# Batch 0's keys in three tiles of 128 and one shared by both heads, instead of four of 112

## The chip, the cores and the metric

The kernel runs on one core of a Trainium2 chip. The metric is the device time of one execution, in microseconds, lower being better. The core has five engines that run their own instructions in order and wait for each other by semaphores: TensorE (PE, matmuls into the PSUM banks; its weight loads are listed as PEld), VectorE (DVE), ScalarE (ACT), GpSimd (POOL) and SyncE (SP), whose queue starts nearly all DMAs.

## What is computed

An attention with soft-capped scores over 4 batches of 12 heads, 448 positions and 64 columns, and behind it two feed-forward layers over the 1792 tokens. All of it is in float32; the cap that comes with the inputs is 30.

```python
def _attn_ref(q, k, v, cap):
    scale = 1.0 / np.sqrt(q.shape[-1])
    scores = scale * np.matmul(q, k.transpose(0, 1, 3, 2))
    scores = cap * np.tanh(scores / cap)
    scores = scores - np.max(scores, axis=-1, keepdims=True)
    attn = np.exp(scores)
    attn = attn / (np.sum(attn, axis=-1, keepdims=True) + 1e-09)
    return np.matmul(attn, v)
...
x = attn_out.transpose(0, 2, 1, 3).reshape(B * S, H * D)
h = x @ moe_w_in                       # 768 to 2048
g = np.where(h >= 1, h, np.where(h <= -1, 0.0, (h + 1) ** 2 / 4))
x = g @ moe_w_out                      # 2048 to 768
h = np.maximum(np.maximum(x @ w1, x @ w2), x @ w3)
return h @ w_out                       # 768 to 768
```

## The kernel before

**Two arms.** Every engine loads the cap's bits into a register (`values_load`, L211) and compares them with a limit (L228). For a cap over 32 the arm with `keep_max=True` runs, which takes the row maxima off the scores; it stands directly behind the comparison. For smaller caps, as here, the arm with `keep_max=False` runs. It has no maxima, stands behind the whole first arm, and is reached by a taken branch of each engine. Each arm holds the full program, over 2,500 rows of it on PE.

**Order of the work.** Inside an arm everything is first noted as operations with a cost, a due time and the buffers they use; the class `Plan` then puts them in an order by these costs and due times, and `emit` writes the instructions in that order. An engine's queue is therefore fixed when the program is built. `slots` says how many buffers each pool has: "u" holds tiles of 896 columns (qk, tanh and exp tiles, sums), "h" those of 448, "v", "wf" (weights as float32) and "raw" (weights as they come) their own; in PSUM there are two score banks "s" (`ps_s`, two banks wide), one "a" and three "m".

**Attention of a pair of heads** (`attention(b, i, ...)`, L571 on, six pairs per batch). SP loads q and k of both heads (`load_heads`, two DMAs of 224 KB) and v (`load_v`, L580, one DMA of 224 KB, 1 KB in a row per key and head). The 448 keys are cut into four tiles of 112. For batch 0 a score tile is four plain float32 matmuls (`score`, L616, matmul in L624): 64 and 48 keys of each head, in four corners of the array at once. ACT turns both heads' scores into tanh (L631, 112x896) and later into exp (L678). DVE adds the four exp tiles into one, `se` (L718, by the helper in L313); PE multiplies that by ones into `ps_r` (`total4`, L707, four products of 224 columns; the last pair uses `total`, L693). PE weighs v with the exp tiles into `ps_a` (`weigh`, L834): four tiles of four products with 32 columns each. For batches 1 to 3 (`FULL`) q and k are divided into two parts each, and a score tile is six faster products (L613).

**Reciprocals.** The row sums leave `ps_r` on DVE or ACT (`rs`, L765 or L763). For all pairs but the last, POOL starts a DMA that gathers them into a small tile `rc` (L786), DVE takes 896 reciprocals there (L807), SP writes them to DRAM (L789) and reads them back, spread over the partitions, into `rs` (L794, two DMAs). Then DVE multiplies `ps_a` by `rs` into `xf` (L313), which frees the bank of `ps_a`, and divides `xf` into two parts `x`. The last pair takes its reciprocals on DVE in four pieces (L818).

**The bank of `ps_a`** is chosen by this line:

```python
pa = buf("m" if first and i % 2 else "a", "ps_a", [P, 512])
```

For batch 0 (`first`) pairs 0, 2 and 4 take the only "a" bank, pairs 1, 3 and 5 one of the three "m" banks, which `ps_r` uses too.

**Feed-forward.** The first layer of batch 0 multiplies `xf` with the first six weight tiles in plain float32 (`PLAIN`, L892), later ones in three products of divided parts (L897 to L899). The weights come as 64-bit words (`raw`, 768 KB a tile) and are turned into float32 by four operations on DVE or ACT (L410 to L437); SP stores them for later use (L443). Attention of batch 1 is mixed into the feed-forward of batch 0, and so on. The last two batches and layers run through L1115.

Of the kernel before, what the change touches and what calls it, by code (L numbers as in the profile page):

```python
# [18 lines left out]
LIMIT_BITS = 0x42000000  # L19

# [184 lines left out]
def kernel(  # L205
# [21 lines left out]
    consts = const, qk0, cap_sb, ones, qscale  # L227
    with tc.If((bits & 0x7FFFFFFF) > LIMIT_BITS) as test:  # L228
# [14 lines left out]
def softcap_attention_two_ffn(  # L243
# [19 lines left out]
    D = 64  # L263
# [7 lines left out]
    FULL = (1, 2, 3)  # L271
    RC = 16
# [11 lines left out]
    slots = {"u": 35, "h": 9, "v": 3, "w": 4, "wf": 5, "raw": 3, "rc": 2, "s": 2, "a": 1, "m": 3}  # L284
    const, qk0, cap_sb, ones, qscale = consts
    dram = pool("dram", 1, space=bass.MemoryType.DRAM)
    pools = {n: pool(n, slots[n]) for n in ("u", "h", "v", "w", "wf", "raw", "rc")}
# [9 lines left out]
    def half(name):  # L297
        return buf("h", name, [P, S])
# [214 lines left out]
    halves = {}  # L513
    def combine(layer, m, run, want):
# [50 lines left out]
    def attention(b, i, begin, last):  # L565
# [7 lines left out]
        vt = buf("v", "v", [C, 2, NCH, D])  # L573
        early = first and i == 0
        qkt = [plan.fixed(qk0) if early else unit("qk")]
        t = [unit("t", rows=C) for _ in range(NCH)]
        if keep_max:
            mx, mb = unit("mx", rows=C), unit("mb", rows=C)
# [27 lines left out]
        for c in range(NCH):  # L606
            ps = buf("s", "ps_s", [P, 2, 512])

            def score_full(e, c=c, ps=ps):
                for n, (k, q) in enumerate(parts3):  # L610
                    for j in range(2):
                        o = slice(j * D, (j + 1) * D)
                        nc.tensor.matmul(  # L613
                            ps.tile[:C, j, :S], k.tile[o, 1, c * C : (c + 1) * C],
                            q.tile[o, 0], start=n == 0, stop=n == 2,
                        )  # L616

            def score(e, c=c, ps=ps):

                for k in (0, D):  # L620
                    n = min(D, C - k)
                    for j in range(2):
                        o = slice(j * D, (j + 1) * D)
# [987 lines left out]
```

## Time and profile before

| | us |
|---|---|
| median of 3 runs | 963.65 |
| lowest and highest run | 961.59, 967.66 |
| the profiled execution | 961.39 |
| its span, first to last recorded instruction | 959.6 |
| PE busy in the span | 939.0 |
| DVE busy | 776.7 |
| ACT busy | 597.2 |

The profile is one execution. The busy time of an engine counts its instructions, not its branches or the starting of DMAs. A float32 matmul stands as two records, so a score tile of four matmuls is "x8". The granted clock (PEclk) is a share of PE's full 2.4 GHz. Idle time of an engine other than the one that sets the pace costs nothing by itself.

### The profile page before, as it was taken

Reading aid. Unit: us, or ns where it says so; the run is one execution under the profiler, and the core shown is the slowest. Engines: PE = TensorE matmul, PEld = TensorE weight load, DVE = VectorE, ACT = ScalarE, POOL = GpSimd, SP = SyncE. Lnnn points to the kernel's source line nnn. Section 1 sums busy time; section 2 is a strip of 40 time slices with the busy share of each in tenths; the row PEclk is TensorE's granted clock in tenths of the full one; section 3 lists DMA queues with packets and bytes.
Section 4 is the critical chain, followed back from the end, with each engine's and each line's share of the span. In section 5 each row is a group of like instructions: output and inputs, shape, how many; then the busy total and the mean of one; then the engine's idle time right before and its main releaser. Section 6 shows DMA issues by size and latency. Waiting matters only on the chain.

```text
span 959.6 us, 14758 instructions
## 1 busy us (share of the span) xinstructions
PE 939.0 (98%) x5323; PEld 755.9 (79%) x5323; DVE 776.7 (81%) x1285; ACT 597.2 (62%) x935; POOL 14.5 (2%) x27
## 2 busy tenths in 40 slices
PE   6889999999999999999999999999999999999998
PEld 1125777777776767677999999999999999899997
DVE  2789898888898898789989848787889869858782
ACT  6798898774989887875434315566874825332441
POOL 0000000000000000000000000000000000000000
PEclk9799999999999999999999999999999999999999
DMA  6667767989998998953777887432333336446344
GB/s 178 208 187 222 236 187 236 268 254 319 304 276 275 270 305 267 270 149 127 251 269 249 294 285 271 151 113 83 104 102 106 110 106 211 130 150 206 101 144 136
DMA packets 95340, 194.49 MB, mean 203 GB/s; under 512 B 12094, under 2 KB 56858, under 8 KB 95258
## 3 DMA queue, kind: packets, MB, share of 16 engines
q1 hardware_dynamic: 94378, 193.36, 64.3%
q8 instruction: 44, 0.72, 0.3%
q14 instruction: 38, 0.31, 0.1%
q0 software_dynamic: 736, 0.10, 0.1%
q10 hardware_dynamic: 144, 0.00, 0.0%
HBM read 142.51 MB, written 50.81 MB: 201 GB/s over the span
## 4 chain that ended last, share of the span: by engine, by line
PE 91%; issue 4%; DMA 2%; DVE 2%; ACT 1%; POOL 0%; POOLq 0%; DVEq 0%; ACTq 0%
PE ps_m L1115 32%; PE ps_s L1115 11%; PE ps_m L897 10%; PE ps_m L899 9%; PE ps_m L898 9%; PE ps_a L834 6%; PE ps_s L613 5%; PE ps_a L1115 5%; PE ps_m L892 3%; PE ps_r L707 1%; DMA rc<-rs 1%; DVE op L313 1%; PE ps_s L624 1%; DMA rc<-rc 0%; DMA qk<-in_qk 0%
## 5 line engine op out<-in xcount | busy, mean ns | idle before, releaser
L1115 PE MATMUL ps_m<-op,w 128*128 128x448 f32 x1575 | 324.1, 365 | 0.5 <-DVE M L313 0.5
L1115 PEld LDWEIGHTS ps_m<-op,w 128*128 128x128 f32 x1575 | 295.6, 188 | 24.5 <-DVE M L313 0.9
L313 DVE TENSOR_TENSOR w<-wf,w 128x512 fp32r<-128x512 f32 (+2 forms) x155 | 117.3, 760 | 13.7 <-ACT w L308 11.4
L308 ACT ACTIVATE w<-wf 128x512 fp32r<-128x512 f32 (+2 forms) x124 | 84.2, 682 | 63.8 <-PE ps_m L1115 30.7
L631 ACT ACTIVATE t<-ps_s,qscale 112x896 f32<-112x896 f32 x96 | 92.7, 1004 | 32.1 <-PE ps_s L613 22.5
L1115 PE MATMUL ps_s<-op,w 128*128 128x448 f32 x522 | 110.7, 366 | 0.4 <-DVE op L313 0.2
L1115 PEld LDWEIGHTS ps_s<-op,w 128*128 128x128 f32 x522 | 98.0, 188 | 8.7 <-ACT op L308 0.5
L678 ACT ACTIVATE t<-t,cap_sb 112x896 f32<-112x896 f32 x96 | 96.4, 1040 | 0.3
L308 ACT ACTIVATE w<-ss 128x384 fp32r<-128x384 f32 (+1 forms) x93 | 53.1, 583 | 64.9 <-PE ps_m L1115 37.4
L834 PE MATMUL ps_a<-t,v 112*32 112x448 f32 (+1 forms) x752 | 83.0, 569 | 1.1 <-DVE xf L313 0.6
L897 PE MATMUL ps_m<-g,w 128*128 128x448 f32 x192 | 72.8, 379 | 0.0
L313 DVE TENSOR_TENSOR w<-ss,w 128x384 fp32r<-128x384 f32 (+1 forms) x98 | 59.7, 626 | 14.4 <-ACT w L308 14.0
L899 PE MATMUL ps_m<-g,w 128*128 128x448 f32 x192 | 70.4, 367 | 0.0
L898 PE MATMUL ps_m<-g,w 128*128 128x448 f32 x192 | 70.3, 366 | 0.0
L834 PEld LDWEIGHTS ps_a<-t,v 112*32 112x32 f32 (+1 forms) x752 | 23.3, 113 | 48.5 <-issue 37.6
L437 DVE SCALAR_TENSOR_TENSOR wf<-raw 128x768 int32<-128x768 int32 (+1 forms) x64 | 55.0, 860 | 5.7 <-ACT raw L429 4.6
L421 DVE SCALAR_TENSOR_TENSOR raw<-raw 128x768 int32<-128x768 int32 (+1 forms) x64 | 55.2, 863 | 4.8 <-ACT raw L410 4.1
L897 PE MATMUL ps_m<-x,w 128*128 128x448 f32 x156 | 58.7, 376 | 0.0
L899 PE MATMUL ps_m<-x,w 128*128 128x448 f32 x156 | 57.0, 366 | 0.0
L898 PE MATMUL ps_m<-x,w 128*128 128x448 f32 x156 | 57.0, 365 | 0.0
L1115 PE MATMUL ps_a<-op,w 128*128 128x448 f32 x234 | 51.3, 365 | 0.0
L313 DVE TENSOR_TENSOR se<-t 112x896 f32<-112x896 f32 x36 | 38.8, 1079 | 12.6 <-ACT t L678 12.6
(142 smaller groups left out, 1424.3 us busy)
## 6 DMA issues: line engine op xcount, KB each, us to landing
wf<-w SPq DMA_DIRECT2D x104, 192.0 KB
wf<-w SPq DMA_DIRECT2D x66, 256.0 KB
w<-wf SPq DMA_DIRECT2D x40, 384.0 KB
wf<-w SPq DMA_DIRECT2D x40, 384.0 KB
raw<-in_w SPq DMA_DIRECT2D x18, 768.0 KB
w<-p SPq DMA_DIRECT2D x36, 384.0 KB
raw<-in_w_in SPq DMA_DIRECT2D x16, 768.0 KB
raw<-in_w_out SPq DMA_DIRECT2D x24, 512.0 KB
```

Of the source, the lines that this page charges most:

```text
L308: nc.scalar.activation(out=out_, in_=in_, func=AF.Copy)
L313: nc.vector.tensor_tensor(out=out_, in0=a, in1=b, op=o)
L421: nc.vector.scalar_tensor_tensor(out=lo, in0=hi, scalar=-(2**31), in1=lo, op0=ALU.bitwise_and, op1=ALU.bitwise_or,)
L437: nc.vector.scalar_tensor_tensor(out=wf.tile[:, :n].bitcast(I32), in0=hi, scalar=3, in1=lo, op0=ALU.logical_shift_left, op1=ALU.bitwise_or,)
L613: nc.tensor.matmul(ps.tile[:C, j, :S], k.tile[o, 1, c * C : (c + 1) * C], q.tile[o, 0], start=n == 0, stop=n == 2,)
L631: nc.scalar.activation(out=t[c].tile, in_=ps.tile[:C, :, :S], func=AF.Tanh, scale=qscale[:C])
L678: lambda e, c=c: nc.scalar.activation(out=t[c].tile, in_=t[c].tile, func=AF.Exp, scale=cap_sb[:C]),
L834: nc.tensor.matmul(pa.tile[j * D + d : j * D + d + n, :S], vt.tile[:, j, c, d : d + n], t[c].tile[:, j], start=start, stop=stop,)
L897: nc.tensor.matmul(ps.tile[:, :S], wh, a.tile[:, 0], start=start, stop=False)
L898: nc.tensor.matmul(ps.tile[:, :S], wh, a.tile[:, 1], start=False, stop=False)
L899: nc.tensor.matmul(ps.tile[:, :S], wl, a.tile[:, 0], start=False, stop=stop)
L1115: nc.tensor.matmul(get(), w_, x_, start=start and z == 0, stop=stop and z == 2, skip_group_check=begun,)
```

## The change

1. The comparison is turned round: the arm for caps up to 32 stands directly behind it, the other one behind that.
2. Batch 0 (`HALVED`) cuts its keys into three tiles of 128 and a last one of 64. The last one holds both heads, head 0 in partitions 0 to 63 and head 1 in 64 to 127, as one tile `th` of 448 columns from pool "h". Its score is two products; its tanh and exp are half as wide.
3. v comes in eight DMAs a pair for batch 0, since the tiles of 128 cross the rows of 112 in DRAM: six for both heads and two for the shared tile, 256 bytes in a row. Three fixed v tiles are cleared once by POOL, so that in the shared tile each head's columns of v are zero in the other head's partitions.
4. The sum of exp: DVE adds three tiles instead of four; PE multiplies both `se` and `th`, the latter by `blocks`, ones in one half of the partitions.
5. `ps_a` of pairs 0 and 3 takes the "a" bank, that of the others an "m" bank.
6. Pool "u" has 34 buffers instead of 35, "h" 11 instead of 9.

The arm for larger caps gets the same tiles; it isn't run with this cap.

```diff
-    bits = nc.values_load(cap.bitcast(I32)[0:1, 0:1])
     const = ctx.enter_context(tc.tile_pool(name="const", bufs=1))
-    qk0 = const.tile([128, 2, qk.shape[4]], F32, name="qk0")
-    load_heads(nc, qk0, qk, 0, 0)
+    qk0 = [const.tile([128, 2, qk.shape[4]], F32, name=f"qk0_{i}") for i in range(FIRST)]
     cap_sb = const.tile([128, 1], F32, name="cap_sb")
     nc.scalar.dma_start(out=cap_sb, in_=cap)
-    ones = const.tile([v.shape[2], 64], F32, name="ones")
+    for i in range(FIRST):
+        load_heads(nc, qk0[i], qk, 0, i)
+    bits = nc.values_load(cap.bitcast(I32)[0:1, 0:1])
+    ones = const.tile([128, 64], F32, name="ones")
     nc.vector.memset(ones, 1.0)
+    blocks = const.tile([128, 2, 64], F32, name="blocks")
+    nc.gpsimd.memset(blocks, 0.0)
+    for j in range(2):
+        nc.gpsimd.memset(blocks[j * 64 : (j + 1) * 64, j], 1.0)
+    vs = [const.tile([128, 512], F32, name=f"v{i}") for i in range(3)]
+    for x in vs:
+        nc.gpsimd.memset(x[:64, 448:], 0.0)
+        nc.gpsimd.memset(x[64:, 384:448], 0.0)
...
+    consts = const, qk0, cap_sb, ones, blocks, vs, qscale
+    with tc.If((bits & 0x7FFFFFFF) <= LIMIT_BITS) as test:
+        softcap_attention_two_ffn(tc, consts, qk, v, *rest, keep_max=False)
+    with test.Else():
         softcap_attention_two_ffn(tc, consts, qk, v, *rest, keep_max=True)
-    with test.Else():
-        softcap_attention_two_ffn(tc, consts, qk, v, *rest, keep_max=False)
 
 
...
+    HALVED = (0,)
...
-    slots = {"u": 35, "h": 9, "v": 3, "w": 4, "wf": 5, "raw": 3, "rc": 2, "s": 2, "a": 1, "m": 3}
+    slots = {"u": 34, "h": 11, "v": 3, "w": 4, "wf": 5, "raw": 3, "rc": 2, "s": 2, "a": 1, "m": 3}
...
+        halved = b in HALVED
+        R = P if halved else C
+        vt = plan.buf("v", lambda: vs[next(v_turn) % len(vs)])
+        early = first and i < FIRST
+        qkt = [plan.fixed(qk0[i]) if early else unit("qk")]
+
+
+        t = [unit("t", rows=R) for _ in range(NCH - 1 if halved else NCH)]
+        th = half("th") if halved else None
...
         def load_v(e):
-            nc.sync.dma_start(
-                out=vt.tile, in_=v[b, 2 * i : 2 * i + 2].rearrange("h p c d -> p h c d")
-            )
+            src = v[b, 2 * i : 2 * i + 2]
+            if not halved:
+                nc.sync.dma_start(
+                    out=vt.tile[:C].rearrange("p (h c d) -> p h c d", h=2, c=NCH),
+                    in_=src.rearrange("h p c d -> p h c d"),
+                )
+                return
+            for k in sorted({*range(0, S, P), *range(0, S, C)}):
+
+                c, p = divmod(k, C)
+                n = min(P - k % P, C - p)
+                part = src[:, p : p + n, c]
+                if k < (NCH - 1) * P:
+                    both = vt.tile[k % P : k % P + n, : 6 * D].rearrange("p (h n) -> p h n", h=2)
+                    o = k // P * D
+                    nc.sync.dma_start(
+                        out=both[:, :, o : o + D], in_=part.rearrange("h p d -> p h d")
+                    )
+                    continue
+                for j in range(2):
+                    o = (6 + j) * D
+                    nc.sync.dma_start(out=vt.tile[head_rows(j), o : o + D], in_=part[j])
+
+        def v_part(j, c, d, n):
+            if halved:
+                o = (3 * j + c if c < 3 else 6 + j) * D + d
+                return vt.tile[:, o : o + n]
+            o = (NCH * j + c) * D + d
+            return vt.tile[:C, o : o + n]
...
+            def score(e, c=c, ps=ps, tail=tail):
+                qk_ = qkt[0].tile
+                for k in (0,) if tail else (0, D):
+                    n = min(D, R - k)
                     for j in range(2):
-                        o = slice(j * D, (j + 1) * D)
+                        to = ps.tile[k : k + n, j, :S] if not tail else ps.tile[head_rows(j), 0, :S]
                         nc.tensor.matmul(
-                            ps.tile[k : k + n, j, :S],
-                            qkt[0].tile[o, 1, c * C + k : c * C + k + n], qkt[0].tile[o, 0],
-                            start=True, stop=True,
+                            to, keys(qk_, j, c, k, n), qk_[head_rows(j), 0], start=True, stop=True
                         )
 
-            def tanh(e, c=c, ps=ps):
+            def tanh(e, c=c, ps=ps, tail=tail):
+                if tail:
+                    nc.scalar.activation(
+                        out=th.tile, in_=ps.tile[:, 0, :S], func=AF.Tanh, scale=qscale
+                    )
+                    return
...
+                    w_, x_ = (blocks[:, j], th.tile) if src is th else (ones[:R], src.tile[:, j])
                     nc.tensor.matmul(
-                        pr.tile[j * D : (j + 1) * D, :S], ones, src.tile[:, j],
-                        start=start, stop=stop,
+                        pr.tile[j * D : (j + 1) * D, :S], w_, x_, start=start, stop=stop
...
+        if halved:
+            se = unit("se", rows=R)
+            sm = add(t[0], t[1], se, w, exps[:2])
+            sm = add(se, t[2], se, w + 0.1, [sm, exps[2]])
+            srcs = [(se, sm), (th, exps[3])]
+        elif ADDED[b] == 0:
...
-        pa = buf("m" if first and i % 2 else "a", "ps_a", [P, 512])
+        pa = buf("m" if first and i % 3 else "a", "ps_a", [P, 512])
```

How the instructions of the arm that runs move, at three places. On PE before, the first three score tiles of pair 3, the sum of pair 2 and the weighing of pair 2 (`ps_s` is a score tile, `se` the summed exp tiles, `t` an exp tile):

```order
L624 MATMUL ps_s<-qk 64x448 [waits DMAHW2_49,Activation_49]
L624 MATMUL ps_s<-qk 64x448 [waits DMAHW3_49]
L624 MATMUL ps_s<-qk 48x448 x2
L624 MATMUL ps_s<-qk 64x448 [waits Activation_49]
L624 MATMUL ps_s<-qk 64x448
L624 MATMUL ps_s<-qk 48x448 x2
L624 MATMUL ps_s<-qk 64x448 [waits Activation_49]
L624 MATMUL ps_s<-qk 64x448
L624 MATMUL ps_s<-qk 48x448 x2
L707 MATMUL ps_r<-se,ones 32x224 [waits DVE_49]
L707 MATMUL ps_r<-se,ones 32x224 x3
L834 MATMUL ps_a<-t,v 32x448 [waits DMAHW1_49,DVE_49]
```

On PE in the changed kernel, from the third weighing of pair 2 to the first of pair 3 (`th` is the shared tile, `v_76` and `v_78` are two of the three fixed v tiles):

```order
L918 MATMUL ps_a<-t,v_78 32x448 [waits DMAHW4_49,DMAHW3_49]
L918 MATMUL ps_a<-t,v_78 32x448 x3
L918 MATMUL ps_a<-th,v_78 32x448 [waits DMAHW5_49,Pool_49]
L918 MATMUL ps_a<-th,v_78 32x448
L918 MATMUL ps_a<-th,v_78 32x448 [waits DMAHW6_49]
L918 MATMUL ps_a<-th,v_78 32x448
L678 MATMUL ps_s<-qk 64x448 [waits Activation_49]
L678 MATMUL ps_s<-qk 64x448 x3
L678 MATMUL ps_s<-qk 64x448 [waits Activation_49]
L678 MATMUL ps_s<-qk 64x448
L918 MATMUL ps_a<-t,v_76 32x448 [waits DMAHW4_49,DMAHW5_49,DVE_49,Activation_49]
L918 MATMUL ps_a<-t,v_76 32x448 x3
```

Before, the weighing of pair 2 is the first that waits for DVE, which is where the bank of pair 0 comes free; now it is the weighing of pair 3, and weighings stand two by two between the score tiles.

On SP before, from the write of pair 0's reciprocals (`rc_0`) to their way back into `rs`:

```order
L789 DMA rc_0_9771<-rc 56x16 [waits DMAHW1_49,DVE_49]
L239 DMA qk<-in_qk 64x2x448 [waits DMAHW2_49]
L239 DMA qk<-in_qk 64x2x448 [waits DMAHW3_49]
L581 DMA v<-in_v 112x2x256 [waits DMAHW4_49,PE_49]
L405 DMA raw<-in_w_in 128x768 [waits DMAHW5_49]
L794 DMA rs<-rc_0_9771 64x448 [waits DMAHW6_49,DMAHW1_49,DMASW0_49]
L794 DMA rs<-rc_0_9771 64x448 [waits DMAHW7_49]
```

On SP in the changed kernel, from behind the write of pair 0's reciprocals to their way back; `v_77` is the v tile of pair 4:

```order
L250 DMA qk<-in_qk 64x2x448 [waits DMAHW6_49]
L250 DMA qk<-in_qk 64x2x448 [waits DMAHW7_49]
L618 DMA v_77<-in_v 112x2x64 [waits DMAHW0_49,PE_49]
L618 DMA v_77<-in_v 16x2x64 [waits DMAHW1_49]
L618 DMA v_77<-in_v 96x2x64 [waits DMAHW2_49,PE_49]
L618 DMA v_77<-in_v 32x2x64 [waits DMAHW3_49]
L618 DMA v_77<-in_v 80x2x64 [waits DMAHW4_49,PE_49]
L618 DMA v_77<-in_v 48x2x64 [waits DMAHW5_49]
L624 DMA v_77<-in_v 64x64 [waits DMAHW6_49,PE_49]
L624 DMA v_77<-in_v 64x64 [waits DMAHW7_49,PE_49]
L417 DMA raw<-in_w_in 128x768 [waits DMAHW0_49]
L878 DMA rs<-rc_0_202 64x448 [waits DMAHW1_49,DMASW0_49]
```

Where one v DMA stood between the write and the way back, eight stand now. A DMA waits for the one eight places before it, whose semaphore it takes over.

On SP before, the end of the arm that runs, behind which nothing but the end of the program stands:

```order
L1008 DMA out_t<-O_18750 128x448 [waits DMAHW2_49,DVE_49]
L1008 DMA out_t<-O_18777 128x448 [waits DMAHW3_49,Activation_49]
L1008 DMA out_t<-O_18790 128x448 [waits DMAHW4_49,Activation_49]
L1008 DMA out_t<-O_18807 128x448 [waits DMAHW5_49,Activation_49]
L228 UNCONDITIONAL_BRANCH
```

On SP in the changed kernel, the end of that arm and the beginning of the other one:

```order
L1093 DMA out_t<-O_9229 128x448 [waits DMAHW5_49,Activation_49]
L1093 DMA out_t<-O_9242 128x448 [waits DMAHW6_49,Activation_49]
L1093 DMA out_t<-O_9259 128x448 [waits DMAHW7_49,Activation_49]
L239 UNCONDITIONAL_BRANCH
L618 DMA v_76<-in_v 112x2x64
L618 DMA v_76<-in_v 16x2x64
L618 DMA v_76<-in_v 96x2x64
```

The arm that runs now ends in a branch over the other arm, of some 670 rows on SP.

## Rows read from the trace of the kernel before

**Rows 1.** The page, busy time of the engines

```profile
PE 939.0 (98%) x5323; PEld 755.9 (79%) x5323; DVE 776.7 (81%) x1285; ACT 597.2 (62%) x935; POOL 14.5 (2%) x27
```

**Rows 2.** Stretches: us; PE, PEld, DVE, ACT, POOL busy; clock, DMA share, GB/s

```profile
7.66:74.59 66.93, 58.43 (x445) 16.64 (x445) 45.60 (x63) 54.08 (x59) 3.16 (x5) 0.90 0.68 200
12.00:17.00 5.00, 4.50 (x41) 1.05 (x40) 2.11 (x2) 4.97 (x7) 0.00 (x0) 1.00 1.08 223
22.50:25.00 2.50, 2.50 (x28) 0.55 (x24) 1.12 (x2) 2.47 (x3) 0.00 (x0) 1.00 1.01 398
...
33.50:43.50 10.00, 8.54 (x48) 1.85 (x48) 7.75 (x12) 4.90 (x6) 0.61 (x1) 0.50 0.66 215
...
56.00:62.00 6.00, 6.00 (x52) 1.83 (x48) 4.52 (x7) 4.25 (x6) 0.12 (x1) 0.72 0.54 186
74.59:956.05 881.46, 880.60 (x4880) 739.22 (x4879) 730.51 (x1219) 541.12 (x874) 11.13 (x18) 1.00 0.65 204
```

**Rows 3.** Chain that ended last, first 110 us: start, us, what

```profile
4.19 3.47 issue
...
19.35 0.42 PE ps_r L707 x8
...
74.59 22.17 PE ps_m L892 x58
```

**Rows 4.** Waits of PE, first 70 us: total, times, longest

```profile
PE ps_s L624 <- ACT t L631: 6.2, 5, 1.8
...
PE ps_a L834 <- DVE xf L313: 0.6, 1, 0.6
```

**Rows 5.** The comparison L228 (min/median/max ns), and SP's first DMA behind it

```profile
L228 PEldq COMPARE_BRANCH  x1: 4958/4958/4958, 2.6 to 2.6; - x1
...
L228 SPq COMPARE_BRANCH  x1: 45/45/45, 4.1 to 4.1; - x1
...
7.04 0.36 SPq L581 DMA_DIRECT2D v<-in_v  x1
```

**Rows 6.** The end: SP's last DMA issues, drains of PE and SP

```profile
951.25 5.72 SPq L1008 DMA_DIRECT2D out_t<-O  x4
...
L1607 SPq DRAIN  x3: 7/7/13, 958.8 to 959.1; - x3
...
L1607 PEldq DRAIN  x2: 13/1923/3833, 952.2 to 959.2; - x2
```

**Rows 7.** PE in order of time, 43 to 49 us: start, us

```profile
43.71 1.72 PE L624 MATMUL ps_s<-qk 64*64 64x448 f32 x16
45.36 3.21 PE L834 MATMUL ps_a<-t,v 112*32 112x448 f32 x32
48.39 0.56 PE L707 MATMUL ps_r<-se,ones 112*32 112x224 f32 x8
48.88 1.35 PE L624 MATMUL ps_s<-qk 64*64 64x448 f32 x12
```

**Rows 8.** Groups by form, first 70 us; the last one 70 to 78 us

```profile
L678 ACT ACTIVATE t<-t,cap_sb 112x896 f32<-112x896 f32 x26 | 26.4, 1040 | 0.3
L631 ACT ACTIVATE t<-ps_s,qscale 112x896 f32<-112x896 f32 x26 | 25.5, 1000 | 9.0 <-PE ps_s L624 8.9
...
L313 DVE TENSOR_TENSOR se<-se,t 112x896 f32<-112x896 f32 x12 | 12.9, 1078 | 4.6 <-ACT t L678 3.6 <-ACT t L631 0.5
...
L308 ACT ACTIVATE x<-xf 128x448 fp32r<-128x448 f32 x2 | 1.1, 574 | 0.0
```

**Rows 9.** Pair 0's reciprocals in order of time: start, us

```profile
20.55 0.74 POOL L786 DMA_DIRECT2D rc<-rs  x1 [20.11 <-DVE rs L765]
...
26.51 0.24 DVE L807 RECIPROCAL rc<-rc 56x16 f32<-56x16 f32 x1 [2.00 <-DMA rc<-rs]
...
37.01 0.62 DVE L313 TENSOR_TENSOR xf<-ps_a,rs 128x448 f32<-128x448 f32 x1 [0.98 <-DMA rs<-rc]
```

**Rows 10.** The page, POOL's DMA queue: packets, MB, share of 16 engines

```profile
q0 software_dynamic: 736, 0.10, 0.1%
```

More of the change, by code (lines that the diff above doesn't have):

```diff
@@ L572, in attention, with head_rows, keys @@
         full = b in FULL
[L573 to L576, printed above, removed]
+        halved = b in HALVED
[5 more added lines that the diff above has]
+        th = half("th") if halved else None
         if keep_max:
-            mx, mb = unit("mx", rows=C), unit("mb", rows=C)
+            mx, mb = unit("mx", rows=R), unit("mb", rows=R)
+        def head_rows(j):
+            return slice(j * D, (j + 1) * D)
         def load_v(e):
-            nc.sync.dma_start(
-                out=vt.tile, in_=v[b, 2 * i : 2 * i + 2].rearrange("h p c d -> p h c d")
-            )
+            src = v[b, 2 * i : 2 * i + 2]
[25 more added lines that the diff above has]
+            return vt.tile[:C, o : o + n]
+        def keys(k, j, c, first=0, n=R):
+            o = c * R + first
+            return k[head_rows(j), 1, o : min(o + n, S)]
         ql = None if early else op(
@@ L639, in attention @@
             else:
-                s = op({"T": SCORE}, score, begin + c * SCORE, [ql], qkt, [ps], "rows")
-            tanhs.append(op({"A": 1.0}, tanh, begin + c * SCORE + 0.5, [s], [ps], [t[c]]))
+                s = op(
+                    {"T": SCORE / 2 if tail else SCORE}, score, begin + c * SCORE, [ql], qkt, [ps],
+                    "rows",
+                )
+            tanhs.append(op(
+                {"A": 0.6 if tail else 1.0}, tanh, begin + c * SCORE + 0.5, [s], [ps],
+                [th if tail else t[c]],
+            ))
         if keep_max:
@@ L649, in attention @@
             )
-            for c in range(2, NCH):
+            for c in range(2, len(t)):
                 m0 = op(
@@ L655, in attention, with larger @@
                 )
+            for j in range(2 if halved else 0):
+                def larger(e, j=j):
+                    o = mx.tile[head_rows(j), j]
+                    tt(e, o, o, th.tile[head_rows(j)], ALU.max)
+                m0 = op(c_tt(KS), larger, w + 0.1, [m0, tanhs[-1]], [mx, th])
             def reduce(e):
@@ L668, in attention, with less @@
         for c in range(NCH):
+            x = th if halved and c == NCH - 1 else t[c]
             sub = tanhs[c]
[L670 removed]
+            if keep_max and x is th:
+                def less(e, x=x):
+                    for j in range(2):
+                        o = x.tile[head_rows(j)]
+                        tt(e, o, o, mb.tile[head_rows(j), j], ALU.subtract)
+                sub = op(c_tt(2 * KS), less, w + 0.1 * c, [ar], [x, mb])
+            elif keep_max:
                 sub = op(
                     c_tt(2 * KS),
[L673 to L674 removed]
+                    lambda e, x=x: tt(e, x.tile, x.tile, mb.tile, ALU.subtract),
+                    w + 0.1 * c, [ar], [x, mb],
                 )
             exps.append(op(
[L677 to L679 removed]
+                {"A": 0.62 if x is th else 1.03},
+                lambda e, x=x: nc.scalar.activation(
+                    out=x.tile, in_=x.tile, func=AF.Exp, scale=cap_sb[: P if x is th else R]
                 ),
[L681 removed]
+                w + 0.1 * c + 0.05, [sub], [x],
             ))
@@ L706, in fn @@
                     o = slice(i % 2 * (S // 2), (i % 2 + 1) * (S // 2))
+                    w_, x_ = ones[:R, :32], src.tile[:, i // 2, o] if src is not th else None
+                    if src is th:
+                        w_, x_ = blocks[:, i // 2, :32], th.tile[:, o]
                     nc.tensor.matmul(
-                        pr.tile[i * 32 : (i + 1) * 32, : S // 2], ones[:, :32],
-                        src.tile[:, i // 2, o], start=start, stop=stop,
+                        pr.tile[i * 32 : (i + 1) * 32, : S // 2], w_, x_, start=start, stop=stop,
                     )
```

44 lines of the change are left out of this document (18 added, 26 removed).

## Prediction

> **What bounds the kernel now.** First the busy shares: TensorE (PE) works 98% of the span [rows 1]. Then the stretches [rows 2]: from 74.59 to 956.05 us PE is busy 880.60 of 881.46 us, so whatever comes earlier moves the end one for one, and only what happens before 74.59 can give much. There, from 7.66 on, PE is idle for 66.93 - 58.43 = 8.5 us, and its clock is granted at 0.50 (1.2 of 2.4 GHz) from 33.5 to 43.5. The chain of waits [rows 3] shows the start: batch 0's first qk is in at 4.19, and PE still does nothing for 3.47 us. The list of PE's waits [rows 4] names ScalarE's (ACT) tanh, which must empty a score bank, and once VectorE's (DVE) xf, which frees the bank of the weighted values.
>
> My mark is the start of the uninterrupted run of plain feed-forward products. Before, 29 of them run from 74.59 in 22.17 us [rows 3], 0.764 each; four others had been done already, so without those the mark would lie at 74.59 - 4 x 0.764 = 71.5. In the new order on PE none stands ahead of the run, and the same four score tiles of batch 1 do. So the new mark compares with 71.5.
>
> **The start.** PE's comparison takes 4.96 us, being taken; SP's ends near 4.15 and its next DMA goes out at 7.04, 2.9 us later [rows 5]. Now the arm stands behind the comparison, and PE can begin when qk lands, at 4.2: 3.5 us gained (bounds 0 and 3.5). The Trainium skill, "Runtime: NRT & Kernel Launch", section "Instruction fetch mechanics", says that a taken branch out of the fetched window must first fetch its target; these rows agree. By that rule the jump is moved rather than removed, since the arm now ends in a branch over the other one.
>
> **The end.** SP issues the last output DMA until 951.25 + 5.72 = 956.97 and drains at 958.8 [rows 6]. Its new jump starts at 956.97 and at 2.9 us, as at the start, ends at 959.9: 1.0 us later than the drain now (bounds 0 and 2.9). PE's sequencer is through at 952.2, when its drain of 3.83 us begins [rows 6]; a jump of 4.96 ends at 957.2, hidden behind SP's.
>
> **The work of a pair of heads.** Two score tiles take 1.65 us, weighing 3.03 / 4 = 0.76 a tile, a switch about 0.14, four sum products 0.49 [rows 7]. Before, a pair was four score tiles, four weighings and four sum products. Now it is three score tiles and a shared one (two products side by side instead of four, so as long as a tile), four weighings and eight sum products, 0.9 us. In the new order PE runs, from pair to pair: two scores, the sum of the pair before, its third and its shared weighing, third and shared score, first two weighings: 1.65 + 0.9 + 1.65 + 1.65 + 1.65 = 7.5 us. On ACT a pair was eight steps of 1.00 to 1.04; now it is six, and two of half size at 0.57 [rows 8]: 7.3 us, less where steps overlap. DVE loses one of three additions of 1.08 [rows 8]. So PE, not ACT, should set the pace, with no wait for a score bank.
>
> Before, pair 0's last weighing ended at 19.35 [rows 3], 11.7 us after PE began. With its sum now ahead of that: 4.2 + 11.7 + 0.7 = 16.6. Two more pairs (15.0) and two score tiles (1.65) bring PE to pair 3's first weighing at 33.3.
>
> **The wait that comes in its place.** Pair 3 takes the bank of pair 0 (before, pair 2 did), so it waits for xf of pair 0, which needs its reciprocals back. Before, that trip ran from POOL's gather at 20.55 over DVE's reciprocal at 26.51 to xf at 37.01 [rows 9]. Now the gather can go at 15.4 and the reciprocal at 21.3; then the trip joins SP's queue, where the v of pairs 3 and 4 stands ahead with eight DMAs each instead of one. Issuing eight costs 8 x 0.36 = 2.9 us [rows 5] and fits into 7.5. The transfers are the question. qk and v run at 223 / 1.08 = 206 GB/s at full share, 12.9 bytes per ns and DMA engine, and raw weights at 398 [rows 2]. So a qk tile of 224 KB is 1.1 us and a raw tile of 768 KB 2.0. v's 224 KB were 224 packets of 1 KB and become 896 of 256 bytes, which no row times. By its bytes at that rate such a packet is 0.020 us, v 1.1 us a pair; if it costs as much as qk's packet of 1792 bytes it is 0.139, v 7.8 us. I take 0.036, v 2.0 us, near the cheap end, because the queue with the smallest packets shows 0.1% x 959.6 x 16 / 736 = 0.021 us for some 140 bytes [rows 10]. Ahead of the reciprocals lie five v (10.0), ten qk tiles (10.9) and three raw (5.9), 26.8 us from 5.5; then their own 1.1 and 1.6 to land: 35.0. xf ends at 35.6, and PE's weighing is 2.4 us late.
>
> DVE works in order. Behind this xf stand 15 instructions up to the last addition for pair 4's sum, then 10 up to pair 5's. At 45.60 / 63 = 0.724 us each [rows 2], and with 0.9 us for pair 1's reciprocals, they end at 35.6 + 10.9 + 0.9 = 47.4 and at 54.6. PE, from 35.7, comes to pair 4's sum at 46.4, 1.0 us too early. From 47.4 it needs 0.9 + 1.65 + 1.65 + 1.65 + 0.7 + 0.8 + 0.7 to pair 5's sum at 55.4, finds it ready, and takes 1.6 + 0.8 + 1.4 more: 59.2. Waits cost clock too: before, 8.54 busy us at 0.50 lost 4.3, and 6.00 at 0.72 lost 1.7 [rows 2]. For two short waits I take the smaller (bounds 0 and 6.0). The mark comes to 60.9.
>
> **Costed at nothing.** POOL's nine clears before its comparison lie in its idle time before its first gather. One wide buffer fewer, two narrow ones more, and the changed order of batch 1's work are hidden while PE never waits behind the mark; now it idles 0.86 us there [rows 2]. If that cover goes, each us of waiting is a us.
>
> **Sum.** Mark 71.5 - 60.9 = 10.6 gained, the start within it; 1.0 given back at the end; net 9.6. The profiled execution took 961.4, which leaves 951.8. It lay 2.3 under the median of the three runs and 0.2 under the lowest; I forecast 952.
>
> **Rivals.**
> *The transfers set the pace, and it turns slower.* At the dear bound six v (46.8), ten qk tiles (10.9), four raw (7.8) and three returns of reciprocals (3.3) must pass, from 5.5, before the last pair is weighed, and some 4.5 us of PE's work follow: 78.8. The end is 961.4 + 7.3 + 1.0 = 970. It is slower than before from a v of 6.4 us a pair on, 0.114 us a packet. For it: one transfer becomes eight, of short packets. Against: the 0.021 us of rows 10. The Trainium skill, "DMA: Bandwidth & Descriptors", section "Rules for kernel authors", says to merge small transfers, since those under 64 KB are mostly overhead; every piece here is under that. From its 0.68 us for 4 KB and 0.95 for 64 KB (section "Bandwidth"), an estimate for eight pieces is 5.4 to 7.6 us a pair, which gives about 955 to 968. No run shows such pieces yet. Chance of ending over 961.4: 0.07.
> *The wait for xf repeats.* If pairs 4 and 5 wait 2.4 us each as well, and the clock takes the larger of its two losses, the mark is 60.9 + 4.8 + 2.6 = 68.3 and the end 959.2. For it: DVE's queue is as full as PE's, and an xf that waits holds the additions behind it. Against: a bank is now held for three pairs, 22.5 us, longer than the trip took before. 0.20 for 955 to 961.
> *No wait at all.* With reciprocals in by 33 the mark is 59.2 - 3.4 = 55.8, the end 946.7. For it: v by its bytes takes 4.5 us off the transfers ahead of them. 0.22 for under 948.
> *The jump was not what held PE.* If the code behind an untaken comparison has to be fetched as well, 3.5 us less are gained: 955.3. Against it: PE's sequencer is recorded inside the comparison for its 4.96 us. 0.05.
> The forecast itself, 948 to 955, has 0.46.
>
> **Numbers.** A measurement of this kernel tells about 1% from no change, here 9.6 us. Faster by over 1% are the case without waits and about half of the forecast's: 0.22 + 0.25 = 0.47. Slower by over 1%, over 971, needs the first rival past its dear end or waits for weights behind the mark: 0.05. The rest, 0.48, lies within 1%. The range is 945 to 961: some 0.1 of the case without waits lies below it, the slower rival above it.
>
> **What would show it.** PE's first product at about 4.2, not 7.66; SP's drain some 2.9 us behind its last issue, not 1.8; pairs 7.5 us apart on PE; one wait of a weighing for xf between 33 and 36; the product run from about 61 on and no idle PE behind it. I am wrong if PE waits for DMAs of v or qk, if pairs are over 9 us apart, or if PE waits for weights after the mark.

## The result: slower, and where the time went

The changed kernel takes 972.94 us (median of 8 runs, 969.45 to 979.29) against 962.59 (8 runs, 958.08 to 967.66): a ratio of 1.0114, 95% interval 1.0081 to 1.0147. The forecast was 952, the range 945 to 961. The profiled execution takes 973.4, its span 971.5. On the page of the changed kernel PE's row by slices shows a place: its second slice, 24 to 49 us, is down to 0.5, from 0.8 before.

```profile
PE   7589999999999999998999999999999999999997
```

PE's five largest waits of the changed kernel over its first 120 us, which answer to [rows 4] (total, times, longest):

```profile
PE ps_r L787 <- DVE se L325: 8.4, 1, 8.4
PE ps_s L678 <- DMA qk<-in_qk: 4.4, 1, 4.4
PE ps_a L918 <- ACT t L755: 2.6, 2, 1.9
PE ps_s L678 <- ACT t L688: 2.5, 1, 2.5
PE ps_m L977 <- DVE xf L325: 1.8, 1, 1.8
```

The 4.4 is only the span's start until the first qk is in. The wait for tanh has shrunk from 6.2 to 3.1 (2.5, and 0.6 for the shared tile's), as meant; that for exp has grown from 0.5 to 2.6. The new one is a single wait of 8.4 us for a *sum* (se), in the third pair (pair 2), two pairs before the first sum that the forecast looked at. PE in order of time (start, us, at the end the wait):

```profile
4.43 6.35 PE L678 MATMUL ps_s<-qk 64*64 64x448 f32 x28 [4.43 <-DMA qk<-in_qk]
...
13.31 1.73 PE L678 MATMUL ps_s<-qk 64*64 64x448 f32 x16
...
20.68 1.74 PE L678 MATMUL ps_s<-qk 64*64 64x448 f32 x16
...
28.04 1.73 PE L678 MATMUL ps_s<-qk 64*64 64x448 f32 x16
38.21 0.97 PE L787 MATMUL ps_r<-se,ones 128*32 128x224 f32 x8 [8.43 <-DVE se L325]
...
73.14 3.27 PE L977 MATMUL ps_m<-xf,wf 128*128 128x448 f32 x8
78.21 22.07 PE L977 MATMUL ps_m<-xf,wf 128*128 128x448 f32 x58 [1.79 <-DVE xf L325]
```

PE starts at 4.43 and runs three pairs 7.4 us apart, both as forecast; then it stands. Who makes the sum late is read from DVE in order of time:

```profile
20.56 1.09 DVE L325 TENSOR_TENSOR se<-se,t 128x896 f32<-128x896 f32 x1
30.08 0.56 DVE L426 TENSOR_SCALAR raw<-raw 128x768 int32<-128x768 uint32 x1 [8.42 <-DMA raw<-in_w_in]
...
33.38 1.08 DVE L325 TENSOR_TENSOR se<-t 128x896 f32<-128x896 f32 x1
36.39 0.56 DVE L426 TENSOR_SCALAR raw<-raw 128x768 int32<-128x768 uint32 x1 [1.93 <-DMA raw<-in_w_in]
...
37.14 1.02 DVE L325 TENSOR_TENSOR se<-se,t 128x896 f32<-128x896 f32 x1
```

The plan put the conversion of the first raw weight tile (L426) ahead of pair 2's first addition, and that of the second tile ahead of its second addition. DVE works in order, so both additions wait for weights that PE needs only 40 us later. The conversion of the first tile stood ahead of pair 2's additions in the kernel before too, but DVE came to it 6.0 us later and found it landed, since SP had started both tiles by 20.7 (SP; DVE; kernel before):

```profile
19.77 0.93 SPq L405 DMA_DIRECT2D raw<-in_w_in  x2
```

```profile
27.63 0.71 DVE L414 TENSOR_SCALAR raw<-raw 128x768 int32<-128x768 uint32 x1
```

Now DVE is ready at 21.65, and the tiles are started at 22.90 and 30.66, the second some 10 us later than before. SP is the reason (start, time in which it issues):

```profile
4.32 2.78 SPq L618 DMA_DIRECT2D v<-in_v  x6
7.21 1.15 SPq L624 DMA_DIRECT2D v<-in_v  x2
...
20.27 2.59 SPq L250 DMA_DIRECT2D qk<-in_qk  x4
22.90 0.59 SPq L417 DMA_DIRECT2D raw<-in_w_in  x1
23.60 3.55 SPq L618 DMA_DIRECT2D v<-in_v  x6
27.25 3.36 SPq L624 DMA_DIRECT2D v<-in_v  x2
30.66 0.58 SPq L417 DMA_DIRECT2D raw<-in_w_in  x1
31.34 0.41 SPq L873 DMA_DIRECT2D rc<-rc  x1
```

Three v, 24 starts, go ahead of the first raw tile; eight take from 4.32 to 8.36, 4.0 us. While they load the first v, the DMA engines have little to do (window; PE, PEld, DVE, ACT, POOL busy; clock, DMA share, GB/s):

```profile
4.00:6.00 2.00, 1.57 (x6) 0.60 (x10) 0.15 (x1) 0.61 (x2) 0.00 (x0) 1.00 0.27 58
6.00:8.00 2.00, 2.00 (x15) 0.57 (x7) 0.00 (x0) 0.89 (x1) 0.00 (x0) 1.00 0.29 64
...
34.00:44.00 10.00, 5.79 (x40) 1.93 (x42) 4.95 (x8) 0.00 (x0) 0.60 (x1) 0.50 0.73 176
```

The last row is what the stall costs on top: the clock is granted at 0.50 (1.2 GHz) from 34 to 44, as before in [rows 2], so 5.79 busy us lose 2.9 more. In the kernel before the same stretch lost 4.3 without such a stall, so the clock is a loss against the forecast, not against the kernel before.

The second raw tile is held in another way too. In the order of SP each DMA waits for the semaphore of the one eight starts ahead of it: the last piece of v has the number that the raw tile had.

```
L417 DMA raw<-in_w_in 128x768 [waits DMAHW3_49]
...
L624 DMA v_76<-in_v 64x64 [waits DMAHW3_49,PE_49]
L417 DMA raw<-in_w_in 128x768 [waits DMAHW4_49]
```

So SP stands at that piece until the first raw tile has landed, and starts the second one only at 30.66. The trace has two such waits of SP at v's last pieces in 62 us, 3.4 us in all, the longer 2.3 (`SPq L624 <- DMA raw<-in_w_in: 3.4, 2, 2.3`). The chain that ended last goes through both tiles (start, us):

```profile
22.90 7.15 DMA raw<-in_w_in
...
30.66 5.70 DMA raw<-in_w_in
```

The first tile takes 7.15 us to land, not the 2.0 that the forecast had for one by itself: four qk starts go right ahead of it, and from 22 to 26 the DMA engines are full (a share of 0.97 and 1.11). So a part of the delay is time in the DMA engines; that SP's late starts pushed these transfers together is argued from the rows, not tested by itself.

Behind the first stage more is lost. A good mark is the end of the first 33 plain products (66 records): before 74.59 + 22.17 = 96.76 [rows 3], after 78.21 + 22.07 = 100.28. The difference of the two profiled spans, 11.9 us, goes:
- until the 33 products have ended: +3.5.
- PE's wait for M where the Strassen part starts, 2.9 for 0.5: +2.4 (first two rows below, changed and before).
- from about 830 on a slower pace of PE, 244 products in 50 us instead of 249 at a granted clock of 1.00 (the two rows behind them): 136 x 5 / 249 = +2.7. Executions of other kernels here, the one before with swapped arms among them, show this pace too, so it is not put down to the change.
- from PE's end to the span's end, 971.5 - 966.27 for 959.6 - 956.03: +1.65.
- 1.6 that nothing in the trace names.

```profile
PE ps_m L1200 <- DVE M L325: 2.9, 2, 2.3
```

```profile
PE ps_m L1115 <- DVE M L313: 0.5, 1, 0.5
```

```profile
750.00:800.00 50.00, 50.00 (x249) 46.34 (x248) 1.00 0.36 107
850.00:900.00 50.00, 50.00 (x244) 45.41 (x243) 1.00 0.51 166
```

At the end (answers to [rows 6]) SP reaches its comparison at 967.3 and drains at 970.7, 3.4 us later; before it was 1.8 from the last issue. The jump is moved, not removed, as the forecast had it.

```profile
L239 SPq COMPARE_BRANCH  x2: 43/46/49, 4.2 to 967.3; - x2
```

```profile
L1692 SPq DRAIN  x3: 7/7/13, 970.7 to 971.0; - x3
```

### The profile page after: what moved, and what is told of

It reads as the page before. It is cut to its first block, busy times and chain, and to the rows that moved or that the text cites. A ratio compares the mean times of both kernels' runs of the same rounds, so it can differ in the third digit from the quotient of the medians.

```text
span 971.5 us, 14877 instructions
## 1 busy us (share of the span) xinstructions
PE 941.9 (97%) x5343; PEld 758.4 (78%) x5343; DVE 772.8 (80%) x1284; ACT 591.3 (61%) x930; POOL 15.8 (2%) x36
## 3 DMA queue, kind: packets, MB, share of 16 engines
q1 hardware_dynamic: 99082, 193.36, 63.4%
## 4 chain that ended last, share of the span: by engine, by line
PE 90%; DMA 3%; SPq 2%; DVE 2%; ACT 1%; issue 1%; DVEq 0%; ACTq 0%
PE ps_m L1200 32%; PE ps_s L1200 11%; PE ps_m L982 10%; PE ps_m L983 9%; PE ps_m L984 9%; PE ps_a L918 6%; PE ps_s L667 5%; PE ps_a L1200 5%; PE ps_m L977 3%; PE ps_r L787 2%; DMA raw<-in_w_in 1%; DMA rs<-rc 1%; DMA rc<-rc 1%; SPq L618 1%; SPq L250 1%
## 5 line engine op out<-in xcount | busy, mean ns | idle before, releaser
L688 ACT ACTIVATE t<-ps_s,qscale 112x896 f32<-112x896 f32 (+1 forms) x90 | 86.9, 1005 | 43.6 <-PE ps_s L667 26.1
L755 ACT ACTIVATE t<-t,cap_sb 112x896 f32<-112x896 f32 (+1 forms) x90 | 89.9, 1038 | 0.2
L918 PE MATMUL ps_a<-t,v 112*32 112x448 f32 (+2 forms) x708 | 74.6, 546 | 2.8 <-ACT t L755 2.6
L918 PEld LDWEIGHTS ps_a<-t,v 112*32 112x32 f32 (+2 forms) x708 | 22.0, 111 | 42.0 <-issue 32.2
L325 DVE TENSOR_TENSOR se<-t 112x896 f32<-112x896 f32 (+1 forms) x36 | 38.9, 1084 | 12.3 <-ACT t L755 12.3
```

Of the source, the lines that this page charges most:

```text
L325: nc.vector.tensor_tensor(out=out_, in0=a, in1=b, op=o)
L688: nc.scalar.activation(out=t[c].tile, in_=ps.tile[:R, :, :S], func=AF.Tanh, scale=qscale[:R])
L755: lambda e, x=x: nc.scalar.activation(out=x.tile, in_=x.tile, func=AF.Exp, scale=cap_sb[: P if x is th else R]),
L918: nc.tensor.matmul(pa.tile[j * D + d : j * D + d + n, :S], v_part(j, c, d, n), t[c].tile[:, j] if c < len(t) else th.tile, start=start, st ...
```

## Experiments

Ratios are to the kernel before, timed beside it on the same chip, where its median was 962.55 to 962.94. A ratio isn't the quotient of two of these medians; the two differ by up to a quarter of a per cent. "33 products" is the mark above, from the profiled run alone. How far it repeats, the pairs show that differ in their buffer counts and have the same first stage otherwise: 96.76 and 97.48, 82.81 and 83.05, but 100.28 and 97.55. A difference of 2 or 3 us in one mark is no more than a hint.

| kernel | 33 products end | ratio, 95% interval | median us |
|---|---|---|---|
| before | 96.76 | | 962.59 |
| changed | 100.28 | 1.0114 (1.0081 to 1.0147) | 972.94 |
| changed, v packed | 82.81 | 0.9920 (0.9878 to 0.9961) | 954.59 |
| before, arms swapped | 94.84 | 0.9958 (0.9927 to 0.9988) | 959.99 |
| before, v in eight | 104.80 | 1.0090 (1.0059 to 1.0122) | 972.86 |
| changed, raw by POOL | 96.50 | 1.0049 (1.0011 to 1.0087) | 969.03 |
| changed, v by POOL | 90.97 | 1.0000 (0.9956 to 1.0043) | 960.57 |
| packed, old counts | 83.05 | 0.9912 (0.9873 to 0.9950) | 952.89 |
| changed, plan told | 91.34 | 1.0071 (1.0024 to 1.0118) | 970.04 |
| before, one v of short packets | 98.55 | 1.0049 (1.0007 to 1.0092) | 968.19 |
| before, new counts | 97.48 | 1.0041 (1.0009 to 1.0073) | 964.81 |
| changed, old counts | 97.55 | 1.0078 (1.0054 to 1.0101) | 969.86 |
| packed, old counts, old arms | 87.31 | 0.9934 (0.9897 to 0.9970) | 954.47 |

Theory: the eight starts a pair on SP are the loss of the first stage. Rivals: the short packets hold the DMA engines; or the two transfers meet in some other way.

### One DMA a pair, everything else as changed

The host lays out batch 0's v in the shape of the tile, zeros included; no arithmetic is moved, and the clears on POOL go.

```diff
-            for k in sorted({*range(0, S, P), *range(0, S, C)}):
...
-                    nc.sync.dma_start(out=vt.tile[head_rows(j), o : o + D], in_=part[j])
+            nc.sync.dma_start(out=vt.tile, in_=v0[i])
```

> The changed kernel, with v of batch 0 laid out ahead in the form of the tiles of 128 (256 KB a pair with the zeros in it), so that one DMA of 2 KB rows replaces eight of 256-byte rows; POOL's clears of v go away. Everything else and the order on PE, DVE and ACT stay. Theory A (SP's time to start DMAs: eight starts hold SP some 4 us a pair, the first raw weights start at 22.90 instead of 19.77, DVE's conversion of them stands ahead of the additions for pair 2's sum, and PE waits 8.4 us for that sum): the first raw weights start by 16, the wait of 8.4 us falls under 2, the run of 29 plain products that began at 78.21 begins between 58 and 66, and the time is 953 to 962, below before. Theory B (the order of PE and DVE in the changed kernel itself, not SP, makes the wait): the wait stays over 5 us, and the time stays over 968. Theory C (short packets fill the DMA engines): as A here; the busy share of the DMA engines while v is loaded tells them apart, 0.3 in the changed kernel by A, over 0.8 by C.

0.992: it beats both kernels. SP starts the first raw tile at 11.45, not 22.90. That is the three v: their starts take 1.4 us together, in the changed kernel 4.0 + 4.2 + 4.9 = 13.1. DVE converts without waiting, PE's waits in the first stage all but vanish, and the clock stays at 1.00 from 34 to 44 (SP; DVE; PE's waits; the same window):

```profile
11.45 0.59 SPq L414 DMA_DIRECT2D raw<-in_w_in  x1
```

```profile
21.50 0.54 DVE L423 TENSOR_SCALAR raw<-raw 128x768 int32<-128x768 uint32 x1
...
27.70 1.09 DVE L322 TENSOR_TENSOR se<-se,t 128x896 f32<-128x896 f32 x1
```

```profile
PE ps_s L661 <- DMA qk<-in_qk: 4.3, 1, 4.3
PE ps_m L960 <- DVE xf L322: 0.7, 1, 0.7
```

```profile
34.00:44.00 10.00, 9.75 (x104) 3.01 (x100) 8.88 (x14) 9.90 (x13) 0.60 (x1) 1.00 0.85 263
```

The plan is the same as in the changed kernel, conversions ahead of additions included; only the weights are there in time. So the order on DVE did no harm by itself: the eight pieces made it harmful. This edit takes away the short packets together with the starts; the next ones part them.

### Eight DMAs in the kernel before

```diff
+            for j in range(2):
+                for c in range(NCH):
+                    nc.sync.dma_start(out=vt.tile[:, j, c], in_=src[:, j, c])
```

> The kernel before with each v load of batch 0 cut into eight DMAs, one for each head and key tile, of 112 rows of 256 bytes; nothing else. By theory A (SP's starts): SP is busy from 7 to about 26 us, the first raw weights start at 25 or later instead of 19.77, DVE waits for them, and the time is 3 to 9 us more than before, with the DMA engines less than half busy while v is loaded. If the number of starts is harmless and only the new order of the work suffers from late weights: within 2 us of before.

The loss comes with the eight pieces alone: 1.009, the 33 products 8.0 us later, the first raw tile started at 30.46 instead of 19.77, and the same two rows, a wait of PE for a sum behind one of DVE for raw weights:

```profile
PE ps_r L711 <- DVE se L313: 6.8, 1, 6.8
```

```profile
DVE raw L414 <- DMA raw<-in_w_in: 7.7, 1, 7.7
```

### Short packets without more starts

In this run the v tile of the kernel before is ordered chunk by head, so its one DMA has rows of 256 bytes, in all four batches.

```diff
-        vt = buf("v", "v", [C, 2, NCH, D])
+        vt = buf("v", "v", [C, NCH, 2, D])
...
-                out=vt.tile, in_=v[b, 2 * i : 2 * i + 2].rearrange("h p c d -> p h c d")
+                out=vt.tile, in_=v[b, 2 * i : 2 * i + 2].rearrange("h p c d -> p c h d")
```

> The kernel before with each v loaded as before by one DMA, but into a tile ordered chunk by head instead of head by chunk, so that its packets are 256 bytes instead of 1 KB (both batches). Theory A (the number of starts counts, not the packets): within 1 us of the kernel before, ratio 0.999 to 1.001, while the same data in eight pieces cost 1.009. Theory B (short packets are the cost): slower by 5 us or more.

Neither theory to the letter: the 33 products end 1.8 us later, and the time's interval, 0.7 to 8.9 us, doesn't settle more. From 8 to 14, with the DMA engines full, short packets move 188 GB/s at a share of 0.95, where the kernel before moves 227 at 0.93 (the first row below is the kernel before, the second this one); so they do cost something where qk competes. Against the 8.0 us of eight pieces it is the smaller part.

```profile
8.00:14.00 6.00, 6.00 (x40) 1.41 (x32) 0.02 (x1) 4.01 (x5) 0.00 (x0) 1.00 0.93 227
```

```profile
8.00:14.00 6.00, 5.93 (x40) 1.35 (x32) 0.15 (x1) 4.73 (x6) 0.00 (x0) 1.00 0.95 188
```

### The raw weights past the eight, and the eight past SP

First, the first two raw tiles started by POOL; second, the v pieces started by POOL; both in the changed kernel.

```diff
+            queue = nc.gpsimd if i < 2 else nc.sync
+            queue.dma_start(out=raw.tile[:, :n], in_=units[i])
```

> The changed kernel with the first two loads of raw weights started by POOL instead of SP; the eight v DMAs a pair stay. By theory A, with the raw weights as the link between SP and PE: they start at about 18 us instead of 22.90 and 30.66, the wait of PE for pair 2's sum falls from 8.4 us to under 3, and the time falls by 4 to 8 us, to 965 to 969; reciprocals still come late, so it does not reach before by much. If SP delays PE by another way (v itself, qk or the reciprocals), the time stays within 2 us of the changed kernel's 973.

The sum's wait falls from 8.4 to 1.0, but the stage gains only 3.8 us, since the next passenger of SP's queue is late instead. Pair 0's reciprocals are ready at 20.2 and written by SP at 29.78. DVE's xf waits 9.5 us for them, and PE stands 8.7 us before pair 3's weighing. The trace names no releaser there ("issue"), but the weighing begins at 43.46, 0.1 us behind the end of that xf. That is the wait that the forecast looked for, not 2.4 but 8.7.

```profile
DVE xf L325 <- DMA rs<-rc: 13.0, 3, 9.5
```

```profile
43.46 3.22 PE L919 MATMUL ps_a<-t,v 128*32 128x448 f32 x16 [8.72 <-issue]
```

```diff
-                    nc.sync.dma_start(
+                    nc.gpsimd.dma_start(
                         out=both[:, :, o : o + D], in_=part.rearrange("h p d -> p h d")
```

> The changed kernel, batch 0's eight v pieces a pair started by POOL's queue instead of SP's; pieces, bytes and tiles stay. Theory A (SP's start time is the cost: eight starts of about 0.5 us a pair ahead of the raw weights and the reciprocals): SP is free again, the first raw load starts near 11 to 13 as in the packed version, the wait for pair 2's sum is under 1.5 us, the product run begins between 61 and 69, total 955 to 964; POOL is busy with starts until about 18, so the first gather goes some 2 us later than 16.8. Theory B (the pieces themselves, short packets and eight completions, hold the data back whoever starts them): waits as in the changed kernel, 969 to 975.

Now the stage ends 9.3 us earlier than in the changed kernel, though not at the packed one's 82.81, and the median is that of the kernel before. SP is free (raw from 9.86), but POOL's queue carries what SP's did: the gather of pair 0's reciprocals stands behind 24 starts and leaves at 23.39, not at 16.8 as in the changed kernel or 2 us behind that as expected. DVE's reciprocal stands ahead of pair 1's second addition, waits 6.0 us, and PE 4.2 for that sum: the same chain with another load in front. The packets don't stay as they were: POOL's queue has 2,272 where it had 736 [rows 10], and SP's 92,938 instead of 99,082, so v goes in 1,536 packets and not in 6,144. This run shows what a free SP is worth and what a full POOL costs; it does not part starts from short packets, which is left to the eight pieces and the one DMA above.

```profile
23.39 0.65 POOL L870 DMA_DIRECT2D rc<-rs  x1 [0.23 <-issue]
```

```profile
25.27 0.24 DVE L891 RECIPROCAL rc<-rc 56x16 f32<-56x16 f32 x1 [6.04 <-DMA rc<-rs]
```

### The plan told what a v costs

```diff
-        vl = op({"Q": 1.0}, load_v, begin + 1, takes=[vt])
+        vl = op({"Q": 4.0 if halved else 1.0}, load_v, begin + 1, takes=[vt])
```

> The changed kernel with one number of the planner changed: a load of v costs SP's queue 4.0 instead of 1.0 for batch 0, which is what its eight starts take. It moves the first reciprocals ahead of pair 3's v, and the first raw load behind them. Theory A (the cost is that the plan did not know of SP's four microseconds; told of them it queues what is due first): no wait of PE for a sum or for xf over 3 us, the product run from 64 to 71, total 957 to 966. Theory B (SP simply has too much to start, 5.3 of 7.4 us a pair, in any order): a wait of 6 us or more returns at another place, 968 to 974.

One number brings the 33 products from 100.28 to 91.34, with all eight starts still on SP: much of the loss lay in the order that the plan made without knowing their cost. The reciprocals go out at 21.06, and the first conversion stands behind pair 2's additions; the raw tiles, first at 30.36, bunch up later (a DMA share of 0.96 from 54 to 64), with one wait of PE of 3.0 for xf. The times are unclear: ten runs lie from 962.88 to 976.69, their median over the 957 to 966 expected, and the profiled one is the lowest. What the number is worth in the stage is shown for that one execution, what it is worth in the median is not.

### The arms, and the buffer counts

The two arms swapped in the kernel before, nothing else:

```diff
-    with tc.If((bits & 0x7FFFFFFF) > LIMIT_BITS) as test:
+    with tc.If((bits & 0x7FFFFFFF) <= LIMIT_BITS) as test:
```

> The kernel before with nothing changed but the order of the two arms. If the jump is what it costs at both ends and the start is passed on: PE begins at 4.4 instead of 7.66, the run of 29 plain products begins some 3 us earlier than 74.59, SP's drain comes 3.5 us behind its last DMA start instead of 1.8, and the time is 1 to 2 us less than before. If the start is swallowed by later waits, because reciprocals and weights do not come earlier: the run begins within 1 us of 74.59 and the time is 1 to 2 us more than before.

PE begins at 4.38 and the 33 products end 1.9 us earlier, of 3 expected; from PE's end to the span's end it is 961.7 - 956.50 = 5.2 instead of 3.6. By these two the swap gains 0.3 us, by the ratio of 0.9958 about 1 to 7; its size stays open. Undone in the packed version, PE begins at 7.36 and the products end 4.3 us later:

> The packed version with the old buffer counts (952.9 where it was timed) and the two arms in their old order. The jump at the start is back and the one at the end gone: PE begins at 7.5 instead of 4.3, the 33 products end 3.3 us later, at 86.3 (less if PE makes some of it up, as in the old kernel where 3.3 became 1.9), and SP drains 1.8 us after its last issue instead of 3.5. Net 0 to 2 us more: 953 to 955. If the jump were nothing in a stage that PE bounds: no later end of the products, and 951.

954.47 against 952.89, within each other's intervals; 4.3 - 1.6 = 2.7 by the two traces. The counts of wide and narrow buffers, alone and taken back:

```diff
-    slots = {"u": 35, "h": 9,
+    slots = {"u": 34, "h": 11,
```

> The kernel before with the new counts of wide and narrow buffers (34 and 11, not 35 and 9), nothing else. Theory A (the counts make PE wait for DVE's M where the Strassen part starts): the wait of 0.5 us becomes 2 to 3, the 33 products end at 96 to 98 as before, total 2 to 4 us more, ratio 1.002 to 1.004. Theory B (the counts matter only together with the new work of the first stage): the wait stays under 1 us, ratio 0.999 to 1.001.

> The changed kernel with the old counts (35 wide, 9 narrow). Theory A: the waits for M of 2.9 us fall under 1, the first stage stays as late as in the changed kernel (the 33 products end at 99 to 102), total 968 to 971, ratio 1.006 to 1.009. Theory B: the waits stay over 2 us and the time at 971 to 973.

> The packed version with the old counts of wide and narrow buffers (35 and 9, not 34 and 11). Theory A (the buffer counts cause the late waits for DVE's M of 2.3 us in the packed version and 2.9 in the changed kernel, against 0.5 before): that wait falls to about 0.5 and the time by 1.8, to a ratio of 0.990 to 0.991. Theory B (the new work order of the first stage shifts the plan, whatever the counts): the wait stays above 1.5 us, ratio 0.992 to 0.993.

The counts are the cause of the waits for M: 0.5 becomes 2.8 in the kernel before, 2.9 becomes 0.9 in the changed one and 2.3 becomes 0.6 in the packed one (in that order):

```profile
PE ps_m L1115 <- DVE M L313: 2.8, 2, 2.3
```

```profile
PE ps_m L1200 <- DVE M L325: 0.9, 1, 0.9
```

```profile
PE ps_m L1183 <- DVE M L322: 0.6, 1, 0.6
```

Two us of a median are at the edge of what these runs resolve; the row of the waits is the evidence. In the changed kernel with the old counts the 33 products end at 97.55, where 99 to 102 were expected: the sum's wait is 6.9 there instead of 8.4, and nothing here says whether the counts or chance did that. The packed version with the old counts has the lowest median here, 952.89, a ratio of 0.9912 (0.9873 to 0.9950), though the intervals of the three packed versions overlap.

## Why the prediction was wrong

Point by point:
- **Start and jump: right.** First product at 4.43 for 4.2. "The jump was not what held PE" falls: 4.38 with the arms swapped alone. The jump at the end cost 1.65 for 1.0.
- **The cycle of a pair: right.** 7.4 us for 7.5, and PE, not ACT, set the pace, for as long as nothing was late.
- **The step that failed:** "Issuing eight costs 8 x 0.36 = 2.9 us [rows 5] and fits into 7.5." Both halves are wrong. The first v's starts take some 0.5 us each, not the 0.36 of the one start that the forecast read, so eight take 4.0. And SP has more in a cycle than eight: two qk starts at 1.29 together, a raw tile at 0.59, the reciprocals at 0.41 and 1.10, together 3.4, so 7.4 in a cycle of 7.4. The queue has no slack left. Besides, it isn't a matter of pace alone: 24 starts and the qk between them hold SP from 4.32 to 22.90, when the first raw tile can start, and DVE wants that tile landed at 21.65. What the runs showed in place of "fits" is PE's wait of 8.4 us for pair 2's sum.
- **What that step hid.** With SP taken as free, the forecast let the *transfers* set when things come, 26.8 us of them in one go from 5.5. They never ran in one go: the share is 0.27 to 0.29 while the first v loads. And the search for a late wait went to xf of pair 0 and the additions of pairs 4 and 5. It did not ask for which DMA each DVE instruction ahead of pair 2's additions waits; two of them were conversions of raw weights. The wait that the forecast named is there in small, behind the large one: xf of pair 0 ends at 46.9 instead of 35.6, and pair 3's weighing begins at 47.01 after 1.9 us of idle time, which the trace puts down to exp tiles that were ready by 46.56.
- **The slower rival: right size, wrong mechanism.** It gave 970 by transfers at 0.139 us a packet, and slower than before from 0.114 on. At 64 GB/s for a share of 0.29, an engine moves 64 / 0.29 / 16 = 13.8 bytes per ns, so a packet of 256 bytes takes about 0.019 us alone, the cheap bound and not the dear one. Its chance of 0.07 was for the wrong reason as well.
- **The rule on small transfers.** The Trainium skill, "DMA: Bandwidth & Descriptors", section "Rules for kernel authors", says to merge small transfers. For this kernel that was the right advice, and the packed version follows it. The trace agrees with the rule and not with reading its price as time of the DMA engines: the price was paid on SP, 4.0 us for the first pair. The forecast's estimate from the Trainium skill's figures was 5.4 to 7.6.
- **Costed at nothing: wrong by 2.4.** One wide buffer fewer and two narrow ones more made PE wait for M at 450 us. The cover named, PE never waiting behind the mark, was thin there already: before, the largest of its waits was this one.

How much hangs on the failed step the packed version tells: with one start a pair, and rows of 2 KB with it, every other step as it was, the products end at 82.81, 17.5 earlier. The forecast's run of 33 from 60.9 would have ended at 60.9 + 33 x 0.764 = 86.1. The trip of the reciprocals, 2.4 late in the forecast, was in time there, and the run began at 56.74: without the eight starts it is the rival "No wait at all" (55.8) that comes close, so the forecast's own wait was too dear by 3.3 at the mark. Against the kernel before the forecast said -9.6 and the profiled run says +12.0. Of the 21.6 between them, 100.28 - 86.1 = 14.2 is the failed step with its lost clock, less those 3.3, 2.4 the counts, 0.65 the jump, 2.7 PE's slower pace in that execution; 1.6 stays open.

So the first idea of the change is sound: three tiles and a shared one, with v in one DMA, the old counts and the old arms, is 0.9934 of the time before.

## What to carry to other kernels

Count starts, not only bytes: when one DMA becomes eight, add up everything that its queue starts in a cycle, at the price that starts have in a full stretch of it, and look at what stands behind it in that queue at the very beginning, where nothing is steady. Then go down each in-order engine that PE waits for, and ask of every instruction ahead of the one needed which DMA it waits for; an instruction that nobody needs yet can hold the one that is needed now. A planner's cost for such a step has to be changed together with the step.

## What the runs showed that was not expected

- A DMA on SP isn't started until the one eight starts ahead of it has landed, by the semaphores in the order and by SP's two waits for raw weights at v's last pieces, 3.4 us. Many small DMAs behind a large one thus make the next large one wait for the first.
- POOL takes 0.52 to 0.67 us for such a start, no less than SP, and its pieces wait for earlier ones too (3.9 and 3.2 us in 45).
- PE has a second pace that the granted clock doesn't show: 244 instead of 249 products in 50 us at 1.00, for hundreds of us in some executions (below, the packed version with old counts, which has 248 from 850 to 900). In that of the changed kernel with old counts it lasts from 500 us at the latest to the end, which is worth 470 x 5 / 249 = 9.4 us. What sets the pace stays open. It is the reason why waits and marks in the traces say more here than medians a few us apart.

```profile
650.00:700.00 50.00, 50.00 (x244) 45.41 (x243) 1.00 0.30 87
```
